# Turning w_out in 32 by 32 blocks on VectorE instead of 128 by 128 on TensorE

## The chip, the cores and the metric

The kernel runs on one core of one Trainium2 chip. The metric is the device time in microseconds (us) of one execution, lower is better. A core has five engines that run their own instruction streams in order and wait for each other by semaphores: TensorE (PE in the profile, with its weight loads shown apart as PEld), VectorE (DVE), ScalarE (ACT), GpSimd (POOL) and SyncE (SP). Here SP does nothing but issue transfers to 16 DMA engines; an "SPq" row is such an issue.

## The reference

```python
# 1. attention with mixing over heads, before and after the softmax: q, k, v are [4, 12, 448, 64]
scores = einsum(scale * q @ k.T, w_pre); attn = softmax(scores); attn = einsum(attn, w_post)
x = (attn @ v) as [1792, 768]
# 2. a wide layer: w_in [768, 2048], w_out [2048, 768]
h = x @ w_in
g = h * cos(h)
x = g @ w_out
# 3. soft mixture: phi [768, 32], 8 experts of 4 slots, w1 [8, 768, 1024], w2 [8, 1024, 768]
logits = x @ phi
d = softmax(logits, over the tokens);  slot_in = d.T @ x
slot_out = per expert: relu(slot_in @ w1) @ w2
out = softmax(logits, over the slots) @ slot_out          # [1792, 768] float32
```

The kernel never forms g @ w_out for all tokens. Logits are g @ (w_out @ phi), so it needs the small product W = w_out @ phi ([2048, 32]), and for that product w_out with its 768 columns on the partitions, that is, turned. The rest of w_out is used only after the sum over the tokens.

## The kernel before

**Phase A** (`phase_a`) is the attention. A planner (`Plan`) with costs and due times sets its order. It also narrows w_in and w_out from their stored form to float32 copies in DRAM. Phase A is untouched by the change.

**Phase B** (`phase_b`) is the wide layer, the logits and the sum over tokens. It takes 1792 tokens in four blocks of 512, 512, 512 and 256, and in each block 16 slices of 128 of the 2048 hidden columns: `body(v)` for v = 0 to 63, written out in a fixed order. "Slice v" below means one `body(v)`. In a slice, `l1(v)` (lines 700 to 710) makes h with 18 matmuls on PE: w_in and x are each split in a high and a low part. The split of the weights for slice v + 2 (`split_w`, lines 650 and 651) is one pass on ACT and one on DVE. `act` and `act2` (lines 717 to 729) make g = h cos(h): ACT line 720, DVE lines 721 and 723, ACT line 728, DVE line 729. `consume` (line 750) turns g of slice v - 2 in 32 by 32 blocks on DVE. After each fourth slice `logits` (line 757) multiplies four g tiles by four tiles of W on PE; that of slices 4i to 4i + 3 stands in slice 4i + 5.

W is made during block 0, in four pieces `fb` of 512 rows of w_out each. The table `more` (line 866) says in which slice which step stands:

- `load_wo(fb)` loads 512 rows of w_out, rows on the partitions.
- `turn_wo(fb, half)` (line 665) turns 384 columns: 12 transposes of 128 by 128 on PE into PSUM (line 672), and three copies of 128 by 512 out of it, on DVE (line 675) or ACT (line 677). There are eight such calls, in slices 1 to 8.
- `mul_phi(fb)` (line 681) multiplies by phi into `pw` on PE; ACT copies it to `ws` (line 690).
- `turn_w(fb)` (line 692) turns the product on PE into a PSUM tile, also called `wtr`, and DVE copies it to `W` (line 697, `wphi` in the profile).

In the table the four `turn_w` stand in slices 4, 6, 8 and 10, and the `logits` that use them in 5, 9, 13 and 17. Steps of `more` come after `split_w` and before `consume`, `logits` and `act2` of the same slice. Block 0 ends with slice 15; the last `logits` of the block is in slice 17.

**Phase C** (`phase_c`) is the experts and the output. It streams w1 and w2 through a ring of buffers; 18 of its 64 units are loaded from slice 16 on, 12 of them into `early`, the same memory that `phase_b` calls `room`.

Of the kernel before, what the change touches and what calls it, by code (L numbers as in the profile page):

```python
# [9 lines left out]
F32 = mybir.dt.float32  # L10
# [9 lines left out]
EARLY, RING, NWF, NWH, LAG = 12, 3, 4, 2, 2  # L20
# [580 lines left out]
def phase_b(tc, st, consts, ident, xT_d, w_in, w_out, phi, sums, room, x0, ahead):  # L601
# [6 lines left out]
    nc = tc.nc  # L608
    SIZES = [512, 512, 512, 256]
    NB = len(SIZES)  # L610
    with ExitStack() as ctx:
# [39 lines left out]
            nc.vector.tensor_tensor(out=wf_t[v], in0=wf_t[v].bitcast(F32), in1=wh.bitcast(F32), op=ALU.subtract)  # L651
            wh_t[v] = wh

        wo_t, wt_t = {}, {}
        ws, ph = room[7][:, :512], room[7][:, 512:704].rearrange("p (c s) -> p c s", c=6)

        def load_wo(fb):
            wo_t[fb] = []
            for i in range(2):
                t = room[2 * (fb % 2) + i].rearrange("p (t d) -> p t d", t=2)  # L660
                r0 = 512 * fb + 256 * i
                nc.sync.dma_start(out=t, in_=w_out[r0:r0 + 256].rearrange("(t p) d -> p t d", p=128))
                wo_t[fb].append(t)

        def turn_wo(fb, half):

            wt = wt_t[fb, half] = room[4 + (2 * fb + half) % 3].rearrange("p (c f) -> p c f", c=3)
            for c in range(3):
                pt = p1.tile([128, 512], F32, tag="tr", bufs=4, name=f"wtr{fb}_{half}_{c}")
                cols = slice(384 * half + 128 * c, 384 * half + 128 * c + 128)  # L670
                for t in range(4):
                    nc.tensor.transpose(pt[:, t * 128:(t + 1) * 128],  # L672
                                        wo_t[fb][t // 2][:, t % 2, cols], ident)
                if c % 2 != half:
                    nc.vector.tensor_copy(out=wt[:, c], in_=pt)
                else:
                    nc.scalar.copy(out=wt[:, c], in_=pt)
            if half and fb + 2 < 4:
                load_wo(fb + 2)

        def mul_phi(fb):
            pw = p1.tile([128, 512], F32, tag="tr", bufs=4, name=f"pw{fb}")
            wt = [wt_t[fb, c // 3][:, c % 3] for c in range(6)]
            for c in range(4):
                nc.tensor.matmul(pw[32 * c:32 * c + 32], ph[:, c, :], wt[c], start=True, stop=False)
            for r in range(4):
                c, cols = 4 + r // 2, slice(256 * (r % 2), 256 * (r % 2) + 256)
                nc.tensor.matmul(pw[32 * r:32 * r + 32, cols], ph[:, c, :], wt[c][:, cols],
                                 start=False, stop=True)
            nc.scalar.copy(out=ws, in_=pw)  # L690

        def turn_w(fb):
# [34 lines left out]
        def act2(h, r):  # L727
            nc.scalar.activation(out=r, in_=r, func=AF.Sin, scale=-2.0 * math.pi, bias=hpi)
            nc.vector.tensor_tensor(out=r, in0=h, in1=r, op=ALU.mult)
# [119 lines left out]
        for part in range(3):  # L849
# [4 lines left out]
        cT, g_acc, z_acc, gn_all, x1, cg = sums  # L854
# [3 lines left out]
        W = sp.tile([128, 16, 32], F32, name="wphi")  # L858
        m_acc = sp.tile([128, 1], F32, name="m_acc")
        magic, hpi = consts[:, 0:1], consts[:, 1:2]  # L860
        nc.sync.dma_start(out=ph, in_=phi.rearrange("(c p) s -> p c s", p=128))
        load_wo(1)

        g_t = {}

        more = {1: [(turn_wo, 0, 0)], 2: [(turn_wo, 0, 1)], 3: [(mul_phi, 0), (turn_wo, 1, 0)],
                4: [(turn_w, 0), (turn_wo, 1, 1)], 5: [(mul_phi, 1), (turn_wo, 2, 0)],
                6: [(turn_w, 1), (turn_wo, 2, 1)], 7: [(mul_phi, 2), (turn_wo, 3, 0)],
                8: [(turn_w, 2), (turn_wo, 3, 1)], 9: [(mul_phi, 3)], 10: [(turn_w, 3)]}


        def body(v):

            b, f = divmod(v, 16)
            last = v - LAG if v - LAG < V - 4 else -1
            pt = l1(v)
            for _ in range(AHEAD_AT.count(v)):
                ahead.pop(0)()
            if v + NWF < V:
                load_w(v + NWF)  # L880
            g_t[v] = act(v, pt)
            if v + 2 < V:
                split_w(v + 2)
            for f_, *x in more.get(v, ()):
                f_(*x)
            if last >= 0:
                after(last)
            act2(*g_t[v])
            if last >= 0:
                soft(last)  # L890
            if f == 0 and b + 1 < NB:
                load_x(b + 1)
            if f in (7, 9, 11) and b + 1 < NB:
                split_x(b + 1, (f - 7) // 2)
# [20 lines left out]
        for v in range(V):  # L915
            body(v)
# [253 lines left out]
@with_exitstack  # L1170
def tile_kernel(ctx: ExitStack, tc: tile.TileContext, q, k, v, w_pre, w_post, w_in, w_out, phi, w1, w2, out):
    nc = tc.nc
    B, H, S, D = q.shape
    const = ctx.enter_context(tc.tile_pool(name="const", bufs=1))
    dram = ctx.enter_context(tc.tile_pool(name="dram", bufs=1, space=DRAM))
    with tc.manual_schedule():
        ident = const.tile([128, 128], F32, name="ident")
        make_identity(nc, ident)
        xT_d = dram.tile([H * D, B * S], F32, name="xT_d")
        wide, narrow = [], []  # L1180
        for i, w in enumerate((w_in, w_out)):
            r = w.shape[0] // 128
            d = dram.tile(list(w.shape), F32, name=f"w32_{i}")
            wide.append((w.rearrange("(p r) f -> p (r f)", p=128),
                         d.rearrange("(p r) f -> p (r f)", p=128)))
            narrow.append(d)
        keep, nexts, sums, loads, rest, wo, gu, x0s = [], [], [], [], [], [], [], []
        xp = ctx.enter_context(ExitStack())

        def start_b():  # L1190
            pool = ctx.enter_context(tc.tile_pool(name="keep", bufs=1, reuse_waits="tile"))

            consts = pool.tile([128, 2], F32, name="consts")
            nc.vector.memset(consts[:, 0:1], MAGIC)
            nc.vector.memset(consts[:, 1:2], math.pi / 2)
            st4 = pool.tile([128, 32], F32, name="st4")
            st = pool.tile([128, 128], F32, name="st")

            early = [pool.tile([128, 1536], F32, name=f"early{i}") for i in range(EARLY)]
            x0 = xp.enter_context(tc.tile_pool(name="x0", bufs=1, reuse_waits="tile")).tile(  # L1200
                [128, 2, 3072], F32R, name="x0")
            nc.vector.tensor_reduce(out=st4, in_=ident.rearrange("p (a s) -> p s a", a=4), axis=AX.X, op=ALU.add)
            nc.vector.tensor_copy(out=st.rearrange("p (a s) -> p a s", a=4),
                                  in_=st4.unsqueeze(1).to_broadcast([128, 4, 32]))
            keep.extend([st, wo, early, gu, rest, xp.close])
            x0s.append(x0)
            nexts.append(phase_b(tc, st, consts, ident, xT_d, narrow[0], narrow[1], phi, sums, early, x0,
                                 loads))
            next(nexts[0])

        phase_a(tc, ident, q, k, v, w_pre, w_post, xT_d, wide, start_b)
        pool = ctx.enter_context(tc.tile_pool(name="sums", bufs=1, side="right", reuse_waits="tile"))

        cg = pool.tile([128, 3072], F32, name="cg")
        sums.append(pool.tile([128, B * S // 128, 32], F32, name="cT"))
        sums.append(pool.tile([128, w_in.shape[1] // 4], F32, name="g_acc"))
        sums.append(pool.tile([128, 1], F32, name="z_acc"))
        gn_all = pool.tile([128, 12288], F32, name="gn")
        x1 = pool.tile([128, 2, 3072], F32R, name="x1")
        sums.extend([gn_all, x1, cg])  # L1220

        early, x0 = keep[2], x0s[0]
        gu.append(cg[:, 1536:3072])
        gu.extend(gn_all[:, c:c + 1536] for c in range(0, 7680, 1536))
        x1s = [x1[:, i, c:c + 768].bitcast(F32) for c in (1536, 2304, 0, 768) for i in range(2)]
        wo.extend(x1s[:4])
        wo.extend(x0[:, i // 4, 768 * (i % 4):768 * (i % 4) + 768].bitcast(F32) for i in range(8))
        wo.extend(x1s[4:])
        first = [(lambda i=i, t=t: load_unit(nc, t, unit_source(w1, w2, i))) for i, t in enumerate(early + gu)]
        rows = [(lambda i=i, t=t: nc.sync.dma_start(out=t, in_=narrow[1][128 * i:128 * i + 128]))  # L1230
                for i, t in enumerate(wo)]
        loads.extend(first[:EARLY] + rows[:12] + first[EARLY:])
        rest.extend(rows[12:])
        for _ in nexts[0]:
            pass
        phase_c(tc, ident, *sums, w1, w2, *keep, out)
# [31 lines left out]
```

## Time and profile before

| | us |
|---|---|
| median of 3 runs | 917.29 |
| lowest and highest run | 914.87 and 920.3 |
| profiled execution, its own time | 911.71 |
| its span, first to last instruction | 909.9 |
| slices 0 to 17, from the first matmul of slice 0 to the first of slice 18 | 498.00 to 596.86 |

The profile is of one execution; all times inside it are from the start of its span. In that execution PE was busy 95% of the span, DVE 68%, ACT 57%. A row of a timeline gives the start, the length, the engine, the line, the operation, and what it writes and reads; a bracket at its end is the idle time of the engine before it and what ended that. Consecutive instructions overlap a little in such rows, so what an instruction costs its engine is read from start to start.

### The profile page before, as it was taken

What the parts mean: (1) busy time and instruction counts of PE and PEld (TensorE: products, weight loads), DVE (VectorE), ACT (ScalarE), POOL (GpSimd) and SP (SyncE); (2) the same over time, 40 slices, a digit from 0 to 9 for tenths busy, and PEclk for the clock granted to TensorE, in tenths of its full rate; (3) what the DMA queues carried; (4) which work ended last, traced back from release to release, by engine and by line L of the source; (5) the groups of instructions that cost most, each with busy time, mean ns of one, the idle gap of its engine ahead of it and who ended that gap; (6) DMA issues with size and microseconds to landing.
All of it is one profiled execution on the core that took longest, in us unless ns stands there. A gap on an engine that the chain in (4) does not pass through costs nothing.

```text
span 909.9 us, 17966 instructions
## 1 busy us (share of the span) xinstructions
PE 866.6 (95%) x6732; PEld 612.4 (67%) x6732; DVE 620.6 (68%) x1282; ACT 519.4 (57%) x1146; POOL 178.8 (20%) x272
## 2 busy tenths in 40 slices
PE   7899999999999999999999999999999999989665
PEld 5567777776777777677778877776777777833112
DVE  4568878688879788778744657777877788833003
ACT  5667767677767678657655545455546457512003
POOL 2233344343434334334310000000000000010000
PEclk9999999999999999999999999999999999999867
DMA  7999896999878997979419732363563358979998
GB/s 167 194 208 246 209 244 203 218 218 276 213 205 224 253 214 177 248 205 250 117 47 289 229 122 70 110 237 129 164 221 132 121 175 276 307 307 414 416 375 314
DMA packets 175474, 198.93 MB, mean 219 GB/s; under 512 B 73424, under 2 KB 147090, under 8 KB 175388
## 3 DMA queue, kind: packets, MB, share of 16 engines
q1 hardware_dynamic: 158504, 159.18, 58.5%
q0 software_dynamic: 14272, 37.96, 18.3%
q8 instruction: 53, 0.87, 0.4%
q10 hardware_dynamic: 2612, 0.65, 0.3%
q14 instruction: 33, 0.27, 0.1%
HBM read 135.40 MB, written 23.59 MB: 175 GB/s over the span
## 4 chain that ended last, share of the span: by engine, by line
PE 81%; DMA 11%; DVE 2%; SPq 1%; issue 1%; ACT 1%; POOL 0%; ACTq 0%; DVEq 0%; POOLq 0%
PE po L444 16%; PE pre L406 15%; PE h L706 9%; PE av L468 8%; PE h L707 8%; PE h L709 8%; PE s L359 8%; DMA early<-in_moe_w_dram 4%; DMA s<-ss 4%; PE p L818 2%; DMA cg<-in_moe_w_dram 2%; DMA ring<-in_moe_w_dram 2%; PE lg L757 1%; PE kt L293 1%; PE wtr L672 1%
## 5 line engine op out<-in xcount | busy, mean ns | idle before, releaser
L444 PEld LDWEIGHTS po<-wc,e 120*112 120x112 f32 x1440 | 170.5, 177 | 56.3 <-issue 41.5
L444 PE MATMUL po<-wc,e 120*112 120x120 f32 x1440 | 182.8, 269 | 0.5 <-ACT am L229 0.5
L406 PE MATMUL pre<-s,kron_pre 120*120 120x448 f32 x360 | 166.5, 552 | 4.6 <-issue 2.7
L409 DVE TENSOR_REDUCE mz<-pre 120x1 f32<-120x448 f32 x180 | 111.1, 620 | 45.6 <-PE pre L406 44.6
L379 POOL DMA_DIRECT2D s<-ss x180 | 107.0, 597 | 174.5 <-ACT ss L229 120.1
L706 PE MATMUL h<-x,wh 128*128 128x512 f32 (+1 forms) x384 | 139.1, 372 | 0.1
L707 PE MATMUL h<-x,wh 128*128 128x512 f32 (+1 forms) x384 | 135.7, 363 | 0.0
L413 ACT ACTIVATE e<-pre,mz 120x448 f32<-120x448 f32 x180 | 114.6, 637 | 29.2 <-DVE mz L409 26.4
L229 ACT COPY am<-po 112x360 f32<-112x360 f32 x190 | 87.4, 461 | 65.3 <-PE po L444 63.3
L706 PEld LDWEIGHTS h<-x,wh 128*128 128x128 f32 x384 | 72.2, 188 | 26.4 <-ACT cg L720 10.0
L709 PE MATMUL h<-x,wf 128*128 128x512 f32 (+1 forms) x384 | 87.3, 363 | 0.0
L720 ACT ACTIVATE cg<-h 128x512 int32<-128x512 f32 (+1 forms) x64 | 34.6, 541 | 90.7 <-PE h L709 89.5
L543 POOL TENSOR_TENSOR nar<-nar,cvt 128x384 uint32<-128x384 uint32 x64 | 64.1, 1001 | 98.1 <-DVE cvt L534 42.0
L468 PE MATMUL av<-am,v 112*64 112x120 f32 (+1 forms) x1536 | 83.0, 262 | 0.0
L468 PEld LDWEIGHTS av<-am,v 112*64 112x64 f32 x1536 | 74.0, 137 | 10.4 <-issue 4.9
L707 PEld LDWEIGHTS h<-x,wh 128*128 128x128 f32 x384 | 72.2, 188 | 11.2
L721 DVE SCALAR_TENSOR_TENSOR cg<-h,cg 128x512 f32<-128x512 f32 (+1 forms) x64 | 39.8, 621 | 57.2 <-ACT cg L720 55.2
L709 PEld LDWEIGHTS h<-x,wf 128*128 128x128 f32 x384 | 66.3, 188 | 11.8
L1037 POOL MEMSET own<- 128x192 f32 x2 | 0.4, 252 | 347.6 <-PE si L1023 347.6
L229 ACT COPY ss<-s 120x448 f32<-120x448 f32 (+1 forms) x104 | 54.1, 532 | 25.0 <-PE s L359 15.5
L406 PEld LDWEIGHTS pre<-s,kron_pre 120*120 120x120 f32 x360 | 53.2, 184 | 21.9 <-issue 16.1
L651 DVE TENSOR_TENSOR wf<-wf,wh 128x768 fp32r<-128x768 f32 x64 | 60.9, 951 | 8.7 <-ACT wh L650 8.7
(174 smaller groups left out, 1223.3 us busy)
## 6 DMA issues: line engine op xcount, KB each, us to landing
s<-ss POOLq DMA_DIRECT2D x144, 210.0 KB, 7.5
early<-in_moe_w_dram SPq DMA_DIRECT2D x36, 768.0 KB
wf<-w SPq DMA_DIRECT2D x64, 384.0 KB
raw<-in_moe_w_in_dram SPq DMA_DIRECT2D x32, 384.0 KB
w<-nar SPq DMA_DIRECT2D x64, 192.0 KB
raw<-in_moe_w_out_dram SPq DMA_DIRECT2D x32, 384.0 KB
gn<-in_moe_w_dram SPq DMA_DIRECT2D x16, 768.0 KB
early<-w SPq DMA_DIRECT2D x8, 768.0 KB
```

The lines of the kernel that those rows point to most:

```text
L229: nc.scalar.copy(out=out, in_=in_)
L359: nc.tensor.matmul(pts[o][:n, :S], x[r, p, :n], y[r, p, :], start=(i == 0), stop=(i == 2))
L379: QUEUE[e].dma_start(out=s2t[ti][h::12, :n // 10], in_=x[o][:n])
L406: nc.tensor.matmul(prt[gi, c][:, :S], kpre, s2t[ti][:, 3 * g + c, :], start=True, stop=True)
L409: nc.vector.tensor_reduce(out=mz[gi][:, 0, c:c + 1], in_=prt[gi, c][:, :S], axis=AX.X, op=ALU.max, negate=True)
L413: nc.scalar.activation(out=et[gi][:, c, :], in_=prt.pop((gi, c))[:, :S], func=AF.Exp, bias=mz[gi][:, 0, c:c + 1], accum_out=mz[gi][:, 1, c ...
L444: nc.tensor.matmul(pt[:, :360].rearrange("p (g i) -> p g i", i=30)[:, :, 10 * c:10 * c + 10], et[gi][:, c, jt * CJ:(jt + 1) * CJ], wct[gi] ...
L468: nc.tensor.matmul(pt[64 * o:64 * o + 64, x * 120:x * 120 + n], vt[:, g, jt, :], am[ti % 2][:, g, jt, :n], start=(jt == 0), stop=(jt == NJ ...
L543: nc.gpsimd.tensor_tensor(out=f, in0=f, in1=x["t"], op=ALU.add)
L706: nc.tensor.matmul(pt, wh[:, c], xh[:, c, :], start=(c == 0), stop=False)
L707: nc.tensor.matmul(pt, wh[:, c], xl[:, c, :], start=False, stop=False)
L709: nc.tensor.matmul(pt, wl[:, c], xh[:, c, :], start=False, stop=(c == 5))
```

## The change

w_out is now turned by DVE in blocks of 32 by 32 and no longer by PE. For such a turn to give w_out with columns on partitions, the load puts column quarter a (192 columns) on partitions 32a to 32a + 31: four transfers for each piece, each to 32 partitions, in runs of 192 elements (768 bytes), where there were two transfers of whole rows (3072 bytes) to all 128 partitions. `turn_wo(fb, x)` is one DVE instruction on 128 by 768; it stands in slice 4 fb + x, after `act2`, so there is one in each of slices 0 to 15. phi is loaded in the matching order, in four transfers. `mul_phi` reads the turned tile with a stride. `mul_phi(fb)` now stands in slice 4 fb + 4 and `turn_w(fb)` in slice 4 fb + 5. The `early` tiles become one tile `room`, with w_out in columns of its own for each piece, and `ws` and `ph` move into a part of `gn_all` that block 0 does not use.

```diff
-        def turn_wo(fb, half):
-            wt = wt_t[fb, half] = room[4 + (2 * fb + half) % 3].rearrange("p (c f) -> p c f", c=3)
-            for c in range(3):
...
-                    nc.tensor.transpose(pt[:, t * 128:(t + 1) * 128],
-                                        wo_t[fb][t // 2][:, t % 2, cols], ident)
-                if c % 2 != half:
-                    nc.vector.tensor_copy(out=wt[:, c], in_=pt)
-                else:
-                    nc.scalar.copy(out=wt[:, c], in_=pt)
-            if half and fb + 2 < 4:
-                load_wo(fb + 2)
+        def load_wo(fb):
+            src = w_out[512 * fb:512 * fb + 512].rearrange("(r i) (a d) -> a i r d", i=32, a=4)
+            for a in range(4):
+                nc.sync.dma_start(out=wo_src(fb)[32 * a:32 * a + 32], in_=src[a])
+        def turn_wo(fb, x):
+            if x == 0:
+                c = 1536 * (8 + 2 * (fb % 2))
+                wt_t[fb] = room[:, c:c + 3072]
+            cols = slice(768 * x, 768 * x + 768)
+            nc.vector.transpose(out=wt_t[fb][:, cols], in_=room[:, 3072 * fb:3072 * fb + 3072][:, cols])
...
+            wt = wt_t[fb].rearrange("p (r c i) -> p c r i", c=6, i=32)
...
-        nc.sync.dma_start(out=ph, in_=phi.rearrange("(c p) s -> p c s", p=128))
-        load_wo(1)
+        ws, ph = gn_all[:, 7168:7680], gn_all[:, 7680:7872].rearrange("p (c s) -> p c s", s=32)
+        for a in range(4):
+            nc.sync.dma_start(out=ph[32 * a:32 * a + 32],
+                              in_=phi[192 * a:192 * a + 192].rearrange("(c j) s -> j c s", j=32))
...
-        more = {1: [(turn_wo, 0, 0)], 2: [(turn_wo, 0, 1)], 3: [(mul_phi, 0), (turn_wo, 1, 0)],
...
+        more = {}
+        for fb in range(4):
+            more[4 * fb + 4] = [(mul_phi, fb)]
+            more[4 * fb + 5] = [(turn_w, fb)]
+        for fb in range(1, 4):
+            more[2 * fb - 1] = more.get(2 * fb - 1, []) + [(load_wo, fb)]
...
             act2(*g_t[v])
+            if v < 16:
+                turn_wo(v // 4, v % 4)
```

On PE before, `turn_w(0)` follows slice 4 and the `logits` that use it follow slice 5 (`h4`, `h5`: the matmuls of these slices; `wtr0_6189`: the PSUM tile of `turn_w`; the other `wtr` tiles: transposes of w_out; `lg0`: the logits).

```order
L709 MATMUL h4_6164<-x0_5873,wf0_5879 128x512 x6
L695 MATMUL wtr0_6189<-st_5857,early7_5865 128x32 x4
L672 MATMUL wtr1_1_0_6195<-ident_62,early2_5860 128x128 x2
...
L709 MATMUL h5_6218<-x0_5873,wf1_5880 128x512 x6
L685 MATMUL pw1_6243<-early6_5864,early7_5865 32x512 x3
...
L672 MATMUL wtr2_0_0_6253<-ident_62,early0_5858 128x128 x2
...
L757 MATMUL lg0_6272<-cg_5967,wphi_5982 32x512 x4
```

On PE of the changed kernel, whose lines from 655 on have smaller numbers (709 is 701, 695 is 687, 757 is 749, 685 is 677), the same stretch holds:

```order
L701 MATMUL h4_6102<-x0_5862,wf0_5868 128x512 x6
L677 MATMUL pw0_6127<-early_5858,gn_5962 32x512 x4
L680 MATMUL pw0_6127<-early_5858,gn_5962 32x256 x4
...
L701 MATMUL h5_6141<-x0_5862,wf1_5869 128x512 x6
L687 MATMUL wtr0_6166<-st_5857,gn_5962 128x32 x4
L749 MATMUL lg0_6177<-cg_5958,wphi_5973 32x512 x4
L698 MATMUL h6_6185<-x0_5862,wh0_5871 128x512
```

The transposes of w_out are gone, `mul_phi` has moved one slice down, and `turn_w` stands directly ahead of the `logits` that read its result.

On DVE before, the copy to W of `turn_w(0)` is in slice 4 (from the reading of `h4` on):

```order
L721 SCALAR_TENSOR_TENSOR cg_5967<-h4_6164,cg_5967 128x512
L723 TENSOR_SCALAR cg_5967<-cg_5967 128x512
L651 TENSOR_TENSOR wf2_5881<-wf2_5881,wh0_5882 128x768
L697 COPY wphi_5982<-wtr0_6189 128x128
L675 COPY early4_5862<-wtr1_1_0_6195 128x512
L675 COPY early4_5862<-wtr1_1_2_6207 128x512
L750 STREAM_TRANSPOSE gn_5971<-cg_5967 128x512
L729 TENSOR_TENSOR cg_5967<-h4_6164,cg_5967 128x512
```

In the changed kernel DVE's slices 3 (its end), 4 (its start) and 5 read as follows; lines 713, 715, 742, 721 and 689 are 721, 723, 750, 729 and 697 of before, and 671 is the new turn.

```order
L742 STREAM_TRANSPOSE gn_5962<-cg_5958 128x512
L721 TENSOR_TENSOR cg_5958<-h3_6069,cg_5958 128x512
L671 STREAM_TRANSPOSE early_5858<-early_5858 128x768
L713 SCALAR_TENSOR_TENSOR cg_5958<-h4_6102,cg_5958 128x512
...
L713 SCALAR_TENSOR_TENSOR cg_5958<-h5_6141,cg_5958 128x512
L715 TENSOR_SCALAR cg_5958<-cg_5958 128x512
L651 TENSOR_TENSOR wf3_5872<-wf3_5872,wh1_5873 128x768
L689 COPY wphi_5973<-wtr0_6166 128x128
L742 STREAM_TRANSPOSE gn_5962<-cg_5958 128x512
L721 TENSOR_TENSOR cg_5958<-h5_6141,cg_5958 128x512
L671 STREAM_TRANSPOSE early_5858<-early_5858 128x768
```

The fourth turn of a piece is DVE's last instruction of a slice, and `mul_phi` on PE needs it one slice later. The copy to W is DVE's fourth instruction of slice 5, behind three that need `h5`.

## Rows read from the trace of the kernel before

**Rows 1.** Slices 0 to 17: length, busy PE, PEld, DVE, ACT, POOL, clock, DMA, GB/s.

```profile
498.00:596.86 98.86, 98.86 (x550) 76.42 (x548) 68.03 (x107) 49.23 (x77) 0.00 (x0) 1.00 0.47 147
```

**Rows 2.** Timeline of PE: start us, us, engine, line, operation.

```profile
498.00 0.50 PE L706 MATMUL h<-x,wh 128*128 128x512 f32 x1
...
524.23 0.97 PE L695 MATMUL wtr<-st,early 128*128 128x32 f32 x8
525.03 1.51 PE L672 MATMUL wtr<-ident,early 128*128 128x128 f32 x12
526.30 0.48 PE L706 MATMUL h<-x,wh 128*128 128x512 f32 x1
...
530.57 1.06 PE L685 MATMUL pw<-early,early 128*32 128x512 f32 x8
...
532.00 1.53 PE L672 MATMUL wtr<-ident,early 128*128 128x128 f32 x12
533.46 1.07 PE L757 MATMUL lg<-cg,wphi 128*32 128x512 f32 x8
534.45 0.50 PE L706 MATMUL h<-x,wh 128*128 128x512 f32 x1
...
538.67 0.97 PE L695 MATMUL wtr<-st,early 128*128 128x32 f32 x8
...
569.83 0.39 PE L706 MATMUL h<-x,wh 128*128 128x512 f32 x1
...
573.91 0.39 PE L706 MATMUL h<-x,wh 128*128 128x512 f32 x1
...
596.86 0.51 PE L706 MATMUL h<-x,wh 128*128 128x512 f32 x1
```

**Rows 3.** Timeline of DVE in slice 4.

```profile
525.05 0.69 DVE L721 SCALAR_TENSOR_TENSOR cg<-h,cg 128x512 f32<-128x512 f32 x1 [2.83 <-ACT cg L720]
...
526.99 0.28 DVE L697 COPY wphi<-wtr 128x128 f32<-128x128 f32 x1
527.19 1.28 DVE L675 COPY early<-wtr 128x512 f32<-128x512 f32 x2
528.39 0.70 DVE L750 STREAM_TRANSPOSE gn<-cg 128x512 f32<-128x512 f32 x1
```

**Rows 4.** Timeline of DVE in slice 15, which has no extra work.

```profile
592.40 0.69 DVE L721 SCALAR_TENSOR_TENSOR cg<-h,cg 128x512 f32<-128x512 f32 x1 [0.98 <-ACT cg L720]
...
594.97 0.65 DVE L729 TENSOR_TENSOR cg<-h,cg 128x512 f32<-128x512 f32 x1
596.60 0.69 DVE L721 SCALAR_TENSOR_TENSOR cg<-h,cg 128x512 f32<-128x512 f32 x1 [0.99 <-ACT cg L720]
```

**Rows 5.** Groups by line, shapes apart: DVE's 32 by 32 turns of g (busy, mean ns).

```profile
L750 DVE STREAM_TRANSPOSE gn<-cg 128x512 f32<-128x512 f32 x48 | 33.8, 703 | 0.0
L750 DVE STREAM_TRANSPOSE gn<-cg 128x256 f32<-128x256 f32 x16 | 6.9, 434 | 0.0
```

**Rows 6.** Timelines of DVE and PEld at a wait of PE for DVE.

```profile
516.35 0.65 DVE L729 TENSOR_TENSOR cg<-h,cg 128x512 f32<-128x512 f32 x1
...
517.30 0.16 PEld L685 LDWEIGHTS pw<-early,early 128*32 128x32 f32 x8 [0.35 <-DVE cg L729]
```

**Rows 7.** Groups by line: matmuls of 512 columns, read with a stride (818) and without (834).

```profile
L818 PE MATMUL p<-gn 32*32 32x512 f32 x384 | 13.4, 597 | 0.0
L834 PE MATMUL ps<-gn,st 128*32 128x512 f32 x30 | 4.7, 604 | 0.1
```

**Rows 8.** Issue of w_out's first piece, DMA totals of 486 to 500 us, end of slice 0 on DVE.

```profile
486.36 0.87 SPq L662 DMA_DIRECT2D early<-w  x2
487.27 1.39 SPq L644 DMA_DIRECT2D wf<-w  x2
...
DMA packets 3565, 4.09 MB, mean 292 GB/s; under 512 B 1014, under 2 KB 2550, under 8 KB 3563
...
508.21 0.69 DVE L729 TENSOR_TENSOR cg<-h,cg 128x512 f32<-128x512 f32 x1 [0.68 <-ACT cg L728]
```

More of the change, by code (lines that the diff above doesn't have):

```diff
@@ L652, in split_w, with wo_src @@
             wh_t[v] = wh
-        wo_t, wt_t = {}, {}
-        ws, ph = room[7][:, :512], room[7][:, 512:704].rearrange("p (c s) -> p c s", c=6)
+        wt_t = {}
+        def wo_src(fb):
+            return room[:, 3072 * fb:3072 * fb + 3072].rearrange("p (r d) -> p r d", r=16)
         def load_wo(fb):
[L658 to L663, printed above, removed]
@@ L665, in turn_wo @@
-        def turn_wo(fb, half):
-            wt = wt_t[fb, half] = room[4 + (2 * fb + half) % 3].rearrange("p (c f) -> p c f", c=3)
-            for c in range(3):
-                pt = p1.tile([128, 512], F32, tag="tr", bufs=4, name=f"wtr{fb}_{half}_{c}")
-                cols = slice(384 * half + 128 * c, 384 * half + 128 * c + 128)
-                for t in range(4):
-                    nc.tensor.transpose(pt[:, t * 128:(t + 1) * 128],
-                                        wo_t[fb][t // 2][:, t % 2, cols], ident)
-                if c % 2 != half:
-                    nc.vector.tensor_copy(out=wt[:, c], in_=pt)
-                else:
-                    nc.scalar.copy(out=wt[:, c], in_=pt)
-            if half and fb + 2 < 4:
-                load_wo(fb + 2)
+            src = w_out[512 * fb:512 * fb + 512].rearrange("(r i) (a d) -> a i r d", i=32, a=4)
@@ L681, in mul_phi @@
+            for a in range(4):
[6 more added lines that the diff above has]
+            nc.vector.transpose(out=wt_t[fb][:, cols], in_=room[:, 3072 * fb:3072 * fb + 3072][:, cols])
         def mul_phi(fb):
             pw = p1.tile([128, 512], F32, tag="tr", bufs=4, name=f"pw{fb}")
-            wt = [wt_t[fb, c // 3][:, c % 3] for c in range(6)]
+            wt = wt_t[fb].rearrange("p (r c i) -> p c r i", c=6, i=32)
@@ L684, in mul_phi @@
             for c in range(4):
-                nc.tensor.matmul(pw[32 * c:32 * c + 32], ph[:, c, :], wt[c], start=True, stop=False)
+                nc.tensor.matmul(pw[32 * c:32 * c + 32], ph[:, c, :], wt[:, c], start=True, stop=False)
             for r in range(4):
-                c, cols = 4 + r // 2, slice(256 * (r % 2), 256 * (r % 2) + 256)
-                nc.tensor.matmul(pw[32 * r:32 * r + 32, cols], ph[:, c, :], wt[c][:, cols],
-                                 start=False, stop=True)
+                c, half = 4 + r // 2, r % 2
@@ L690, in mul_phi @@
+                nc.tensor.matmul(pw[32 * r:32 * r + 32, 256 * half:256 * half + 256], ph[:, c, :],
+                                 wt[:, c, 8 * half:8 * half + 8], start=False, stop=True)
             nc.scalar.copy(out=ws, in_=pw)
@@ L860, in phase_b @@
         magic, hpi = consts[:, 0:1], consts[:, 1:2]
-        nc.sync.dma_start(out=ph, in_=phi.rearrange("(c p) s -> p c s", p=128))
-        load_wo(1)
+        ws, ph = gn_all[:, 7168:7680], gn_all[:, 7680:7872].rearrange("p (c s) -> p c s", s=32)
+        for a in range(4):
+            nc.sync.dma_start(out=ph[32 * a:32 * a + 32],
+                              in_=phi[192 * a:192 * a + 192].rearrange("(c j) s -> j c s", j=32))
         g_t = {}
-        more = {1: [(turn_wo, 0, 0)], 2: [(turn_wo, 0, 1)], 3: [(mul_phi, 0), (turn_wo, 1, 0)],
-                4: [(turn_w, 0), (turn_wo, 1, 1)], 5: [(mul_phi, 1), (turn_wo, 2, 0)],
-                6: [(turn_w, 1), (turn_wo, 2, 1)], 7: [(mul_phi, 2), (turn_wo, 3, 0)],
-                8: [(turn_w, 2), (turn_wo, 3, 1)], 9: [(mul_phi, 3)], 10: [(turn_w, 3)]}
+        more = {}
[4 more added lines that the diff above has]
+            more[2 * fb - 1] = more.get(2 * fb - 1, []) + [(load_wo, fb)]
         def body(v):
@@ L1197, in start_b @@
             st = pool.tile([128, 128], F32, name="st")
-            early = [pool.tile([128, 1536], F32, name=f"early{i}") for i in range(EARLY)]
+            room = pool.tile([128, EARLY * 1536], F32, name="early")
+            early = [room[:, 1536 * i:1536 * i + 1536] for i in range(EARLY)]
             x0 = xp.enter_context(tc.tile_pool(name="x0", bufs=1, reuse_waits="tile")).tile(
@@ L1206, in start_b @@
             x0s.append(x0)
-            nexts.append(phase_b(tc, st, consts, ident, xT_d, narrow[0], narrow[1], phi, sums, early, x0,
+            nexts.append(phase_b(tc, st, consts, ident, xT_d, narrow[0], narrow[1], phi, sums, room, x0,
                                  loads))
```

## The prediction

> **What bounds the kernel now.** I read the summary of the page first (PE busy 95% of the span), then the chain of work that ended last, which through phase B is a string of PE's own matmuls, and then the stretch that the change touches: slices 0 to 17, from the first matmul of slice 0 to the first of slice 18. The busy times by stretch [rows 1] show PE busy in all 98.86 us of it, at the full granted clock of 1.00, with DVE at 68 us, ACT at 49 us and the DMA engines at 0.47. So what PE is rid of there is worth its whole length, unless PE begins to wait. From slice 18 on the order of all engines is the same in both kernels, and the loads for phase C hang on slice numbers; a shift at slice 18 arrives at the end as it is. I forecast that shift.
>
> **What PE is rid of, and what is left.** The reader is to see four lengths on PE's timeline [rows 2]. A slice that follows a slice takes 573.91 - 569.83 = 4.08 us. One that follows other work takes longer: 538.67 - 534.45 = 4.22, so 0.14 more (the one from 526.30 to 530.57 takes 4.27, part of it a short wait). `turn_w` takes 525.03 - 524.23 = 0.80, `mul_phi` 532.00 - 530.57 = 1.43, `logits` 534.45 - 533.46 = 0.99. The twelve transposes of one `turn_wo` take 526.30 - 525.03 = 1.27; there are eight calls, about 10.2 us. With the transposes gone the stretch holds 18 slices at 4.08 = 73.4, eight entries after other work or after the start at 0.14 = 1.1, and four times 1.43 + 0.80 + 0.99 = 12.9: together 87.4 us. If PE never waited, the change would be worth 98.9 - 87.4 = 11.4 us (the transposes, and fewer entries and short waits around them).
>
> **What DVE gets.** Eight calls of `turn_wo` gave DVE twelve copies of about 0.60 each, from start to start (the two in [rows 3] take 528.39 - 527.19 = 1.20). They go: 7.2 us. Sixteen turns of 128 by 768 come. The trace has turns of 512 and 256 columns at 0.703 and 0.434 us [rows 5]; another 256 columns cost 0.269, so 768 cost 0.97, and 0.89 from start to start, as rows overlap by some 0.08. Bounds: not under 0.70, the price of 512 columns, and not over 1.41, two turns of 512. Sixteen are 14.2 us. In a plain slice DVE's own work takes from 592.40 to 594.97 + 0.65, 3.22 us, and it idles 0.98 in a period of 4.20 [rows 4]. The turn fits that hole almost exactly: DVE needs 4.1 us a slice against PE's 4.08. It becomes as full as PE in plain slices, but not more; the time that PE spends on `mul_phi`, `turn_w` and `logits` lets it catch up. ACT loses twelve copies, which is worth nothing, since it idles anyway.
>
> **The two new waits on PE.** The order on PE and DVE shows them, the trace prices them. Let T be the moment when PE has finished a slice's matmuls and goes on.
>
> The second wait is the large one. In slice 4 fb + 5 PE does `turn_w`, and directly behind it `logits`, which read the W that DVE must first copy out. DVE cannot be early with that copy: it stands behind line 721 (713 now), which reads this same slice's h. In slice 4 of before, T is 524.23, line 721 starts at 525.05 (0.82 after T, since ACT's line 720 comes between), and the copy to W runs from 526.99 to 527.27, 3.04 after T [rows 2, 3]. DVE idled before it, so this is the shortest it can be. From DVE's end to PE's start I add 0.2: the trace has one such wait, 0.30 from 517.00 to 517.30 [rows 6], which is the upper bound; the lower is 0. PE's own `turn_w` covers 0.80 of it. PE stands idle 3.04 + 0.20 - 0.80 = 2.44 us, four times. Before, the copy had a slice or more between it and its reader. Queued behind the waiting `logits` are all of PE's later slices.
>
> The first wait: `mul_phi(fb)` follows the matmuls of slice 4 fb + 4 and needs the fourth turn of its piece, DVE's last instruction of slice 4 fb + 3. With T of that slice, DVE starts at T + 0.82, works 3.22 less an overlap of 0.07, and turns for 0.97: done at T + 4.94, seen at T + 5.14. PE is there at T + 4.08. It waits 1.06, if DVE has no lag. Lag comes from the splits of x on DVE (slices 7, 9 and 11, after the turn) and from the start of the phase; the idle 2.44 us of PE let DVE recover before each next group, so I take none.
>
> Together 3.50 a group, 14.0 for four (12.4 with no hop, 14.8 with 0.30). The stretch becomes 87.4 + 14.0 = 101.4, against 98.9: **2.5 us slower**. Of the forecast's own uncertainty, the turn's price moves the first wait one for one (0.27 less at 0.70, 0.44 more at 1.41, and in that last case a lag as well), and a lag of 2 us from slice 0 would lengthen the first of the four.
>
> **Edits at no cost.** The strided reading in `mul_phi`: 597 ns for strided and 604 for plain matmuls of 512 columns [rows 7]; at most 0.1 us either way. The load of phi now waits for the last use of phase A's memory and holds SP's queue up to about 498; the load behind it is that of slice 4's weights, which needs slice 0 finished at about 502 anyway, and if that cover were gone there are still two slices until it is needed. Issues: SP has eight more for w_out (16 against 8) and three more for phi, at 0.87 for two [rows 8], 4.8 us spread over six slices, in which SP mostly waits for PE to free a weight buffer; without that cover each would delay the weights of a slice by 0.44, which are loaded four slices ahead. The second piece of w_out is no longer loaded ahead of phase A's last stores, which can let slice 0's ACT work start earlier; PE does not wait for that, so zero.
>
> **Time.** The profiled execution took 911.71 us (span 909.9); with 2.5 more, 914.2. The median of the runs, 917.29, is 5.6 above it, so the runs should give 917.29 + 2.5 = 919.8. About 0.5% (4.6 us) is what a measurement of this kernel can tell from no change.
>
> **Rivals.** (a) *PE does not wait.* Then all 11.4 us are gained: 905.9. For it: PE bounds the stretch without a gap [rows 1], and DVE has 30 us idle. Against it: W is read directly behind its making, and the copy cannot precede line 721 of the same slice. If only the wait before `logits` were much shorter than read, say 1 us, the gain is 3 us, still within the 0.5%. I give it 0.08. The Trainium skill, "VectorE: DVE Perf Modes", section "Rules for kernel authors", says that for a 32 by 32 turn DVE's transpose is the fastest path; taken as the whole story it argues for (a). The trace agrees on the instruction (0.97 us of DVE by my working for what takes PE half of 1.27 us and 1.5 copies), but the rule prices the engines' work and not the waits.
>
> (b) *The quarter loads come late.* The first piece, 1.57 MB, is issued from 486.36 on, in a stretch that moves 292 GB/s [rows 8]: 5.4 us, landed at about 493. The first turn would stand at the end of slice 0 on DVE, behind line 729 of 508.21 [rows 8], or some 2 us earlier if ACT starts earlier. At half the rate it lands at about 498, at a quarter at about 508: the rival decides from there. Beyond that DVE stalls at its first turn with everything of slices 1 and on behind it, the weights of slices 2 and 3, issued behind w_out, come late too, and PE, which can run about two slices ahead, stops. At a sixth of the rate (32 us, 519) DVE is 10 us late and PE some 6, and the later pieces cost as much again: 919.8 + 8 = 928. Against it: the rate would have to fall far. Chance 0.12. The Trainium skill, "SBUF — State Buffer", section "Door 1: The DMA port swizzle (why `[64,N]` ≈ `[32,N]`)", says that a transfer to 32 partitions reaches only 8 of the 16 ports, and that two transfers to different partitions do not add up. By that rule the piece would take about twice as long, 11 us as an estimate, and land at about 498; no row before shows a load to 32 partitions.
>
> (c) *The turn is dearer than its columns*, near 1.3 us. DVE then needs 4.4 us in a slice, falls 0.3 behind in each, and the first wait of each group grows by about 0.35 + 1.0: four times that is 5 us more, 924.9. Nothing in the rows speaks for it but that 768 columns do not occur. Chance 0.10.
>
> **Chances.** Forecast 0.70, (a) 0.08, (b) 0.12, (c) 0.10. The forecast's 2.5 us lies under the 4.6 of the bound; with its spread and that of the runs (914.87 to 920.3) I split its 0.70 into 0.02 faster, 0.56 same and 0.12 slower. With (a) faster, (b) slower and (c) 0.04 same and 0.06 slower: faster 0.10, same 0.60, slower 0.30. The forecast alone spans 916 to 924; with part of (b) and (c) the range is 912 to 926.
>
> **What would show it.** In the profile after: no PE transposes of w_out; sixteen turns of 128 by 768 on DVE near 0.97; PEld idle before the `logits` of slices 5, 9, 13 and 17, released by DVE's copy to W, about 2.4 each; PE idle before `mul_phi`, released by the turn, about 1.1 each; slice 18 some 101.4 us after slice 0. It is wrong if PE has no gap there, if the turn misses 0.97 by over 0.2, if DVE waits for a DMA at a turn, or if phase C differs by more than the shift.

## The result, and the profile after

The changed kernel took 929.71 us (median of 4 runs, 928.5 to 930.41) against 918.79 for the kernel before (4 runs, 914.87 to 922.0): ratio 1.0122, 95% interval 1.0084 to 1.0159. It is 1.2% slower, about 11 us; forecast were 2.5 us, and the time lies above the stated range.

The profiled execution starts slice 0 at 504.70, not at 498.00. Phase A is the same program in both, and over the twelve kernels told of here that start lies between 498.0 and 506.2 without regard to the change. So all comparisons below are made from the first matmul of slice 0 to the first of slice 18, the stretch of [rows 1]. From slice 18 to the end before takes 313.0 us and after 314.6; the other kernels here, with the same order in that part, take 313.0 to 317.5.

Busy time by stretch of the changed kernel (columns as in [rows 1]): the whole stretch, and two pieces behind its first `logits`, in slices 6 and 7.

```profile
504.70:613.65 108.95, 95.37 (x455) 69.97 (x453) 76.85 (x115) 44.29 (x66) 0.00 (x0) 0.94 0.67 158
539.06:543.96 4.90, 4.90 (x16) 3.89 (x13) 0.15 (x1) 0.00 (x0) 0.00 (x0) 0.55 1.18 223
544.00:548.00 4.00, 4.00 (x19) 3.34 (x18) 1.81 (x3) 1.98 (x3) 0.00 (x0) 1.00 1.13 192
```

The stretch is 10.1 us longer than in [rows 1]. PE is idle for 108.95 - 95.37 = 13.6 us of it, where it was never idle before, and the mean granted clock is 0.94, where it was 1.00. Behind the first `logits` the clock is 0.55 for 4.9 us and then 1.00 again. What PE waited for in the stretch (total us, times, longest):

```profile
PE lg L749 <- DVE wphi L689: 10.0, 4, 3.6
PE pw L677 <- DVE early L671: 3.5, 4, 1.2
```

These are the two waits of the forecast and no other. PE's timeline (columns as in [rows 2]) from the `mul_phi` of slice 4 into slice 6, and then the later `logits` with the first matmul behind each:

```profile
526.60 1.07 PE L677 MATMUL pw<-early,gn 128*32 128x512 f32 x8 [1.19 <-DVE early L671]
...
528.03 0.50 PE L698 MATMUL h<-x,wh 128*128 128x512 f32 x1
...
530.89 1.52 PE L701 MATMUL h<-x,wf 128*128 128x512 f32 x6
532.50 1.08 PE L687 MATMUL wtr<-st,gn 128*128 128x32 f32 x8
537.20 1.94 PE L749 MATMUL lg<-cg,wphi 128*32 128x512 f32 x8 [3.62 <-DVE wphi L689]
539.06 0.80 PE L698 MATMUL h<-x,wh 128*128 128x512 f32 x1
539.65 0.63 PE L699 MATMUL h<-x,wh 128*128 128x512 f32 x1
540.08 0.63 PE L698 MATMUL h<-x,wh 128*128 128x512 f32 x1
...
543.49 0.40 PE L698 MATMUL h<-x,wh 128*128 128x512 f32 x1
543.73 0.40 PE L699 MATMUL h<-x,wh 128*128 128x512 f32 x1
543.96 1.52 PE L701 MATMUL h<-x,wf 128*128 128x512 f32 x6
...
560.04 0.97 PE L687 MATMUL wtr<-st,gn 128*128 128x32 f32 x8
563.15 1.19 PE L749 MATMUL lg<-cg,wphi 128*32 128x512 f32 x8 [2.13 <-DVE wphi L689]
564.26 0.80 PE L698 MATMUL h<-x,wh 128*128 128x512 f32 x1
...
568.56 1.54 PE L701 MATMUL h<-x,wf 128*128 128x512 f32 x6
...
587.85 1.93 PE L749 MATMUL lg<-cg,wphi 128*32 128x512 f32 x8 [2.13 <-DVE wphi L689]
589.71 0.80 PE L698 MATMUL h<-x,wh 128*128 128x512 f32 x1
...
593.30 1.53 PE L701 MATMUL h<-x,wf 128*128 128x512 f32 x6
...
612.65 1.07 PE L749 MATMUL lg<-cg,wphi 128*32 128x512 f32 x8 [2.13 <-DVE wphi L689]
613.65 0.50 PE L698 MATMUL h<-x,wh 128*128 128x512 f32 x1
```

Read the starts. Behind the first wait the `logits` take 539.06 - 537.20 = 1.86 us, where [rows 2] have 0.99, and a matmul of 512 columns starts every 0.43 (539.65 to 540.08); from 543.49 on it is 0.24. Nothing about these instructions has changed but the clock: 1.2 GHz instead of 2.4. It happens behind three of the four waits; behind the fourth the `logits` take 1.00.

DVE ahead of that first `logits`, from the turn to the copy to W, and then two of its rows ahead of the second:

```profile
534.07 0.96 DVE L671 STREAM_TRANSPOSE early<-early 128x768 f32<-128x768 f32 x1
534.96 0.65 DVE L713 SCALAR_TENSOR_TENSOR cg<-h,cg 128x512 f32<-128x512 f32 x1
535.64 0.43 DVE L715 TENSOR_SCALAR cg<-cg 128x512 uint32<-128x512 uint32 x1
535.99 0.95 DVE L651 TENSOR_TENSOR wf<-wf,wh 128x768 fp32r<-128x768 f32 x1
536.86 0.28 DVE L689 COPY wphi<-wtr 128x128 f32<-128x128 f32 x1
...
560.87 0.69 DVE L713 SCALAR_TENSOR_TENSOR cg<-h,cg 128x512 f32<-128x512 f32 x1 [1.42 <-ACT cg L712]
...
562.81 0.28 DVE L689 COPY wphi<-wtr 128x128 f32<-128x128 f32 x1
```

In the first group DVE is late and has no gap; the copy stands fourth in its slice, as read from the order. PE, with its product ready at about 533.6, waits for the copy at 536.86. In the second group DVE had been idle 1.42 us, so it is not late; the copy ends at 563.09 and `logits` start at 563.15. Of the three instructions ahead of the copy only two need the h of this slice: line 651 splits the weights of a later one and stands there by order alone. No run here puts the copy ahead of it.

### The profile page after: what moved, and what is told of

It reads as the page before. It is cut to its first block, busy times and chain, and to the rows that moved or that the text cites. A ratio compares the mean times of both kernels' runs of the same rounds, so it can differ in the third digit from the quotient of the medians.

```text
span 928.2 us, 17766 instructions
## 1 busy us (share of the span) xinstructions
PE 867.9 (94%) x6636; PEld 609.2 (66%) x6636; DVE 626.9 (68%) x1286; ACT 513.5 (55%) x1134; POOL 179.1 (19%) x272
## 4 chain that ended last, share of the span: by engine, by line
PE 76%; DMA 11%; DVE 6%; SPq 3%; ACT 2%; issue 1%; DVEq 0%; ACTq 0%
PE po L444 15%; PE pre L406 14%; PE av L468 8%; PE h L698 7%; PE h L699 7%; PE s L359 7%; PE h L701 6%; DMA knat<-in_k_dram 4%; DMA early<-in_moe_w_dram 3%; PE eh L1060 2%; DMA wf<-w 2%; PE p L810 2%; DMA ring<-in_moe_w_dram 2%; PE lg L749 2%; DVE wf L651 2%
## 5 line engine op out<-in xcount | busy, mean ns | idle before, releaser
L698 PE MATMUL h<-x,wh 128*128 128x512 f32 (+1 forms) x384 | 142.6, 381 | 0.0
L699 PE MATMUL h<-x,wh 128*128 128x512 f32 (+1 forms) x384 | 138.8, 371 | 0.0
L698 PEld LDWEIGHTS h<-x,wh 128*128 128x128 f32 x384 | 74.6, 194 | 30.2 <-issue 8.0
L699 PEld LDWEIGHTS h<-x,wh 128*128 128x128 f32 x384 | 74.6, 194 | 11.7
```

The costliest lines, as they stand in the source:

```text
L698: nc.tensor.matmul(pt, wh[:, c], xh[:, c, :], start=(c == 0), stop=False)
L699: nc.tensor.matmul(pt, wh[:, c], xl[:, c, :], start=False, stop=False)
```

## The experiments

The theory after the result: the waits are as forecast, and the half clock that follows them is the rest of the loss. Two rivals: the rest comes from the late quarter loads, or from DVE, which is full of turns. All medians stand beside runs of the kernel before on the same chip (917.52, 917.08 and 917.29 in the three groups).

**The wait kept, PE kept busy in it.** Behind `turn_w` PE turns the identity 18 times into an unused PSUM tile.

```diff
-            more[4 * fb + 5] = [(turn_w, fb)]
+            more[4 * fb + 5] = [(turn_w, fb), (fill, 18)]
```

> The changed kernel, with 18 transposes of the identity into a spare PSUM tile put on TensorE between turn_w and the logits that wait for W (slices 5, 9, 13 and 17; about 2 us of work in a wait of 2.1 to 3.6). Theory (clock): the wait itself costs some 13.5 us in all, and the rest of the loss is TensorE at half clock after three of these waits (6.8 + 3.4 + 3.4 us at a granted clock of 0.5, half of which is lost). With TensorE busy in the wait the clock stays at 1.0, the time falls by about 7 us, from 930 to 923, and no slice of slices 5 to 18 has matmuls of 0.43 us. Rival (loads): the rest of the loss comes from weights that arrive late behind the quarter loads of w_out; then filling the wait changes nothing, 929 to 931.

921.11 us, ratio 1.0037 (0.9993 to 1.0080). The stretch:

```profile
498.62:600.35 101.73, 97.07 (x526) 74.23 (x525) 76.99 (x115) 44.51 (x66) 0.00 (x0) 1.00 0.70 170
```

PE's timeline in slice 5 of this kernel:

```profile
525.74 0.97 PE L687 MATMUL wtr<-st,gn 128*128 128x32 f32 x8
526.55 2.16 PE L864 MATMUL fill<-ident 128*128 128x128 f32 x18
530.04 1.06 PE L749 MATMUL lg<-cg,wphi 128*32 128x512 f32 x8 [1.33 <-DVE wphi L689]
531.04 0.50 PE L698 MATMUL h<-x,wh 128*128 128x512 f32 x1
```

The `logits` still cannot start before the copy to W (4.30 us from `turn_w`, 4.70 in the changed kernel), but the clock stays at 1.00, and the stretch is 7.2 us shorter. It is 101.73, where the forecast's sum at full clock was 101.4. Loads and turns of this kernel are those of the changed one, so neither rival can account for the 7.2, but for some 0.9 by which waits are shorter: 0.40 here, and 0.5 before the four `mul_phi` (2.9 in all, 3.5 in the changed kernel). The other 6.3 us are the clock.

**The new places with the old turns.** The kernel before, its steps put where the change puts them.

```diff
...
+        for fb in range(4):
+            more[4 * fb + 2] = [(turn_wo, fb, 0)]
+            more[4 * fb + 3] = [(turn_wo, fb, 1)]
+            more[4 * fb + 4] = [(mul_phi, fb)]
+            more[4 * fb + 5] = [(turn_w, fb)]
```

> The kernel before with w_out turned on TensorE as before, but with the steps where the change puts them: turns in slices 4fb+2 and 4fb+3, mul_phi in 4fb+4, turn_w in 4fb+5, directly ahead of the logits that read its result. Theory (placement and clock): four waits of 2.3 us before the logits, 9 us, and about 7 us of half clock after them, although nothing is turned on VectorE and nothing is loaded by quarters: 919 + 16 = 935, slower than the changed kernel. Rival (loads): only the 9 us of waits, 928, and the clock stays at 1.0. Rival (VectorE's turns or the quarter loads make the whole loss): 919.

932.24 us, ratio 1.0169 (1.0115 to 1.0223), stretch 112.63, clock 0.95. PE's waits in it, and two of its `logits`:

```profile
PE lg L757 <- DVE wphi L697: 8.5, 4, 2.1
```

```profile
537.74 1.94 PE L757 MATMUL lg<-cg,wphi 128*32 128x512 f32 x8 [2.13 <-DVE wphi L697]
...
565.57 1.06 PE L757 MATMUL lg<-cg,wphi 128*32 128x512 f32 x8 [2.13 <-DVE wphi L697]
```

Whole rows in two loads a piece, no turn of w_out on DVE, and still the wait of 2.13 and the half clock: the placement alone does it. The stretch is 3.7 us longer than in the changed kernel: PE still makes the transposes, while `mul_phi` does not wait and a spell at half clock is missing. The wait is the same 2.13 before both rows, and only the first is followed by half clock. What decides between them is open.

**One slice earlier.** The changed kernel, with `mul_phi` and `turn_w` one slice up and the turns moved up to suit (two in slice 1), so that the copy to W has a slice before its reader.

```diff
-            more[4 * fb + 4] = [(mul_phi, fb)]
-            more[4 * fb + 5] = [(turn_w, fb)]
+            more[4 * fb + 3] = [(mul_phi, fb)]
+            more[4 * fb + 4] = [(turn_w, fb)]
...
-            if v < 16:
-                turn_wo(v // 4, v % 4)
+            for i in [0] if v == 0 else [1, 2] if v == 1 else [v + 1] if v < 15 else []:
+                turn_wo(i // 4, i % 4)
```

> The changed kernel with all its steps one slice earlier: turn 0 in slice 0, turns 1 and 2 in slice 1, turn i in slice i - 1 from then on, mul_phi in 4fb+3, turn_w in 4fb+4, so that the copy to W has a slice before the logits. Theory (placement and clock): the four waits before the logits (10.0 us) and the half clock after them (6.8 us) go, the wait before mul_phi (3.5 us) stays: 930 - 17 = 913, faster than before. Rival (loads): the waits go, but weights still come late and the first turn of the next piece now meets its load, so 919 to 922, with VectorE waiting for DMAs. If the order had nothing to do with it: 930.

915.82 us, ratio 0.9974 (0.9938 to 1.0010); stretch 95.82. The wait of `logits` is gone. 915.82 cannot be told from the kernel before. Left is the wait of `mul_phi`, and behind its longest, 2.44, PE is at half clock again (clock 0.98):

```profile
PE pw L677 <- DVE early L671: 5.2, 4, 2.4
```

**The load in another cut.** Sixteen transfers of 32 rows to all 128 partitions, in place of four to 32 partitions.

```diff
-            for a in range(4):
-                nc.sync.dma_start(out=wo_src(fb)[32 * a:32 * a + 32], in_=src[a])
+            for r in range(16):
+                r0 = 512 * fb + 32 * r
+                nc.sync.dma_start(out=wo_src(fb)[:, r], in_=w_out[r0:r0 + 32].rearrange("i (a d) -> a i d", a=4))
```

> The changed kernel with each piece of w_out loaded in 16 transfers of 32 rows to all 128 partitions instead of four transfers of 512 rows to 32 partitions each; the runs of 768 bytes and the place of everything stay. Theory (placement and clock): the loads cost only the late weights of slice 6 (first wait before logits 3.6 instead of 2.1 us), so about 1.5 us less, 928, and that only if transfers to 128 partitions are faster; the waits and the half clock stay. Rival (loads to 32 partitions run at half rate and this makes the rest of the loss): DMA engines move w_out at 300 GB/s and more instead of about 200, and the time falls by 7 us, to 922. If the rate hangs on the 768-byte runs, it stays at 200 GB/s and 930.

965.77 us, ratio 1.0530 (1.0468 to 1.0592); stretch 146.61. It failed as a cure, against the 922 to 930 expected, and shows what a really late load costs: PE waits 12.4 us for weights and 20.1 for ACT's copy of `pw`, ahead of which ACT stands for weights too. The DMA engines at 492 to 506 us (totals, then the sync engine's queue: packets, MB, share of 16 engines):

```profile
DMA packets 1572, 1.21 MB, mean 87 GB/s; under 512 B 65, under 2 KB 1568, under 8 KB 1568
...
q1 hardware_dynamic: 1549, 1.15, 27.3%
```

A good quarter of the engines' time (27.3%) is used, and the rate is 87 GB/s. The Trainium skill, "DMA: Bandwidth & Descriptors", section "Why a DMA increments its semaphore by 16 and not by 1", says that a transfer uses the largest number of engines up to 16 that divides the slowest dimension of both of its sides; the source here begins with 4. The trace agrees.

**Turns ahead of the slice's other steps.** As one slice earlier, but the turn stands right behind `split_w`, ahead of `more`.

```diff
+            for i in [0] if v == 0 else [1, 2] if v == 1 else [v + 1] if v < 15 else []:
+                turn_wo(i // 4, i % 4)
             for f_, *x in more.get(v, ()):
...
-            if v < 16:
-                turn_wo(v // 4, v % 4)
```

> The changed kernel with its steps one slice earlier (as in the run before) and, on VectorE, each turn put right behind the split of the weights, ahead of the turn of g and the last product of the slice. Theory (placement and clock): the last turn of a piece now ends some 0.3 us before TensorE asks for it, so the waits before mul_phi (5.2 us in the run with the steps one slice earlier, 1.7 us of half clock behind the longest) shrink to what the load of the second piece causes: 916 - 5 = 911, faster than the kernel before by 0.5 to 1%. Rival (VectorE is now the bound): the products that release TensorE's PSUM come 0.9 us later in each slice, TensorE waits for them, no gain: 916 or more.

914.44 us where 911 was expected, ratio 0.9960 (0.9934 to 0.9986); stretch 94.19. The wait of `mul_phi` falls to one of 1.4; now one `logits` waits 2.2, behind a turn for which DVE waited 5.0 for its load, and half clock follows it.

**The loads further apart.** The same, with the loads of pieces 1 to 3 in slices 0, 3 and 7, where they stood in 1, 3 and 5.

```diff
-            more[2 * fb - 1] = more.get(2 * fb - 1, []) + [(load_wo, fb)]
+            at = {1: 0, 2: 3, 3: 7}[fb]
+            more[at] = more.get(at, []) + [(load_wo, fb)]
```

> As the run with early turns, with the loads of pieces 1, 2 and 3 in slices 0, 3 and 7 instead of 1, 3 and 5. Theory (placement, clock, and loads only as a small term): no wait of VectorE for a load and no wait of TensorE in slices 0 to 17 is left, the stretch takes 87.5 to 88.5 us against 98.9 before, granted clock 1.00 in it, and the time is 918 - 11 = 907. Rival (the loads keep all DMA engines busy from slice 0 to 8 at half rate and weights come late wherever they stand): the stretch keeps waits for weights, 911 or more.

916.26 us where 907 was expected, ratio 0.9968 (0.9937 to 0.9999); stretch 93.78. No gain over the last: one wait of 2.9 is left, of `turn_w` for ACT, and ACT itself stood 6.7 for a slice's weights, queued behind other loads. Half clock follows here too, but only about 2 us after PE has resumed:

```profile
525.28 1.08 PE L687 MATMUL wtr<-st,gn 128*128 128x32 f32 x8 [2.95 <-ACT gn L682]
...
527.82 0.63 PE L698 MATMUL h<-x,wh 128*128 128x512 f32 x1
```

**Partition groups alone.** The kernel before, each load of w_out cut in four by partitions, rows still whole.

```diff
-                nc.sync.dma_start(out=t, in_=w_out[r0:r0 + 256].rearrange("(t p) d -> p t d", p=128))
+                src = w_out[r0:r0 + 256].rearrange("(t p) d -> p t d", p=128)
+                for a in range(4):
+                    nc.sync.dma_start(out=t[32 * a:32 * a + 32], in_=src[32 * a:32 * a + 32])
```

> The kernel before, its loads of w_out (whole rows, runs of 3072 bytes) cut in four transfers, each to a group of 32 partitions. It tells what halves the rate of the loads in the changed kernel. If the 32 partitions do: while w_out's first piece moves, all DMA engines are busy at about 190 GB/s. If the 768-byte runs do: 300 to 400 GB/s, as before. Time: as before, 916 to 921, by either, since TensorE has the piece only to use from slice 1 on; 925 if late weights cost much.

Its result stands beside that of the next run.

**Short runs alone.** The kernel before, each load cut in four by columns, 768-byte runs to all 128 partitions.

```diff
+                    nc.sync.dma_start(out=t[:, :, 192 * a:192 * a + 192], in_=src[:, :, 192 * a:192 * a + 192])
```

> The kernel before, its loads of w_out cut in four transfers by column quarters: runs of 768 bytes, each transfer to all 128 partitions. If the 768-byte runs halve the rate: about 190 GB/s while the first piece moves; if the 32 partitions do: 300 GB/s or more. Time: as before, 916 to 921.

918.12 us, ratio 1.0006 (0.9977 to 1.0035), and 918.13, ratio 1.0006 (0.9981 to 1.0031); stretches 98.87 and 99.89 (in the second PE waits once, 0.8 us, for weights). No cost in time that could be measured, but the rates differ. DMA totals while w_out moves, in the kernel before (489 to 492) and with partition groups (497 to 500):

```profile
DMA packets 432, 1.20 MB, mean 399 GB/s; under 512 B 23, under 2 KB 46, under 8 KB 432
```

```profile
DMA packets 273, 0.68 MB, mean 228 GB/s; under 512 B 55, under 2 KB 55, under 8 KB 272
```

Groups of 32 partitions, with the same long runs, bring 399 GB/s down to 228; short runs alone to 274 (489 to 493); the changed kernel, with both, moves 203 (495 to 503). The forecast's rule of the Trainium skill ("SBUF — State Buffer", "Door 1: The DMA port swizzle (why `[64,N]` ≈ `[32,N]`)") agrees with the first.

**Earlier, and the loads out of each other's way.** As with the loads further apart, but in slices 0, 4 and 8, and the load of x for block 1 in slice 3 and not 0.

```diff
-            at = {1: 0, 2: 3, 3: 7}[fb]
+            at = {1: 0, 2: 4, 3: 8}[fb]
...
-            if f == 0 and b + 1 < NB:
+            if f == (0 if b else 3) and b + 1 < NB:
```

> As the run with spread loads (steps one slice earlier, turn behind the split), with the load of x for block 1 moved from slice 0 to slice 3 and w_out's pieces 1, 2, 3 loaded in slices 0, 4 and 8. In the run with spread loads ScalarE waited 6.7 us for the weights of slice 6, which stood in the DMA queues behind x and a quarter-loaded piece; TensorE then waited 3 us for ScalarE's copy of pw and ran at half clock for 3.4 us: 93.8 us for slices 0 to 17. Theory: these are the only losses left, so the stretch takes 88 to 89 us at a granted clock of 1.00, 10 less than before, and the time is 907 to 909 (ratio 0.989 to 0.992). Rival (half-rate loads make weights late wherever they stand): some wait for weights stays in the stretch, 92 us or more, ratio 0.996 as in the last two.

910.18 us, ratio 0.9922 (0.9893 to 0.9952): faster than both kernels, by a little less than expected. The stretch, and PE around slice 5:

```profile
502.45:591.91 89.46, 88.94 (x454) 66.06 (x452) 72.69 (x110) 42.14 (x63) 0.00 (x0) 1.00 0.74 175
```

```profile
524.68 0.97 PE L687 MATMUL wtr<-st,gn 128*128 128x32 f32 x8
525.49 0.48 PE L698 MATMUL h<-x,wh 128*128 128x512 f32 x1
...
529.75 1.06 PE L749 MATMUL lg<-cg,wphi 128*32 128x512 f32 x8
```

A slice now lies between `turn_w` and `logits`, and one wait of 0.5 is left in the whole stretch. 89.46 is 2.1 us above the forecast's 87.4 for a PE that never waits; 0.5 of that is the wait.

**The spread loads alone.** The changed kernel with that load of x, and pieces 1 to 3 in slices 0, 5 and 9.

```diff
-            more[2 * fb - 1] = more.get(2 * fb - 1, []) + [(load_wo, fb)]
+            at = {1: 0, 2: 5, 3: 9}[fb]
+            more[at] = more.get(at, []) + [(load_wo, fb)]
...
```

> The changed kernel with every step where the change has it, only its loads are spread: x for block 1 in slice 3, w_out's pieces 1, 2, 3 in slices 0, 5 and 9. It sizes the late weights by themselves. Theory (placement and clock): the first wait before the logits is 2.1 us as the other three, instead of 3.6; the other waits and the half clock after some of them stay; the stretch takes 107 us and the time is 928. Rival (loads): the stretch comes near 101, the sum without clock and late loads, 922.

930.61 us, ratio 1.0122 (1.0085 to 1.0160), stretch 108.05, clock 0.95: the time of the changed kernel. PE's waits:

```profile
PE lg L749 <- DVE wphi L689: 8.5, 4, 2.1
PE pw L677 <- DVE early L671: 6.2, 4, 3.9
```

ACT ahead of that 3.9:

```profile
519.49 0.83 ACT L650 CAST wh<-wf 128x768 fp32r<-128x768 f32 x1 [3.39 <-DMA wf<-w]
```

All four waits of `logits` are now 2.13, so the 3.62 of the changed kernel's first was the loads (ACT stood 5.1 us there for a slice's weights). But weights are late here too, one slice earlier: ACT stands 3.39, DVE's turn behind it is late, and one wait of `mul_phi` is 3.90 instead. So this run moves the long wait and does not remove it. What the changed kernel would take with no late weights at all, no run here shows.

## Why the forecast was wrong

*What PE is rid of: right.* No transpose of w_out is left on PE. Without waits and at full clock the stretch takes 89.46, one wait of 0.5 in it; forecast 87.4.

*The turn: right.* In the groups by line of the changed kernel, beside [rows 5]:

```profile
L671 DVE STREAM_TRANSPOSE early<-early 128x768 f32<-128x768 f32 x16 | 15.3, 959 | 0.0
```

0.96 us where 0.97 was worked out, so rival (c) is out.

*The two waits: right in cause and place, near in size.* The profile has 3.62 once and 2.13 three times before `logits`, and 0.71 to 1.19 before `mul_phi`: 13.5 us of idle time. The forecast's 14.0 is counted from start to start, and in that measure the ends of PE's rows come on top, 1.4 us (worked out below): 14.9. Without lag, `logits` start 563.15 - 560.04 - 0.80 = 2.31 after the end of `turn_w`, where 2.44 was forecast: the copy ends 3.05 after T, as forecast (3.04), but the hop to PE is 0.06 and not 0.20. The excess is the lag in the first wait, 1.5 us, a term that the forecast put at nothing. Rival (a) is out by the same rows.

*The step that failed: the sum, "87.4 + 14.0 = 101.4".* It took every matmul at the length it has in [rows 2], that is, at the full clock of a PE that is never idle, and then put idle time between them. In the rows above, three spells at half clock cost: `logits` 0.87, 0.12 and 0.87 over 0.99; the slice behind them up to line 701 takes 4.90, 4.30 and 3.59, where one at full clock takes 2.86 (528.03 to 530.89), so 2.04, 1.44 and 0.73. That is 6.1 us. With it the sum is 87.4 + 13.5 + 6.1 = 107.0 of 108.95. Of the last 1.9, some 1.4 are the ends of PE's rows, which the next matmul covers only where there is no wait (`turn_w` takes 0.97 ahead of a wait and 0.80 without, 0.17 in each of eight); 0.5 stays unexplained. Keeping PE busy in the wait gives 101.73, so the step is shown by a run and not only argued. None of the three rivals held this case: all priced a wait at its own length.

*Rival (b): right in the rate, wrong in its weight.* The loads run at about half rate. What that does to the queue is in SP's issues and one split on ACT, in the changed kernel:

```profile
513.61 6.22 SPq L663 DMA_DIRECT2D early<-w  x4
519.94 4.73 SPq L644 DMA_DIRECT2D wf<-w  x2
```

```profile
531.13 0.83 ACT L650 CAST wh<-wf 128x768 fp32r<-128x768 f32 x1 [5.08 <-DMA wf<-w]
```

The four issues of a piece, costed at 1.7 us (twice the 0.87 of [rows 8]), take 6.2 here, the weights of a slice are issued behind them, and ACT waits 5.1 for weights: the source of the 1.5 us of lag above. Spreading the loads in the changed kernel moved that lag and left the stretch at 108.05. With the steps one slice earlier, spreading them brought it from 93.78 to 89.46.

*Edits at no cost: right but for one.* Groups and short runs in the kernel before cost nothing that could be measured there, and the strided matmuls of `mul_phi` take 1.07 for eight where [rows 2] have 1.06. Only the eight more issues on SP had a price, the one just told.

## What to carry to other kernels

Where TensorE is the bound and has been busy throughout, price a new wait on it at its length plus what may follow at half clock; here 13.5 us of waits took about 6 us more with them. Work taken off the bounding engine pays only if what it feeds is made early: the change with W read directly behind its making was 1.2% slower. A slice between the two made up for the loss (ratio 0.9974, not to be told from the kernel before); 0.8% faster came only with the turn earlier in its slice and the loads moved apart as well. If a step cannot be moved, matmuls whose result nobody reads can keep the clock up in the wait; here they did.

## What the hardware showed that was not expected

- In slices 0 to 17 half clock came behind waits of 2.1 us and more (up to 3.9, but for the run with sixteen transfers, which has longer ones), and behind none of 1.4 or less. It did not come behind each of 2.1: behind three of four in the changed kernel, and behind one wait of 2.13 and not another in the same run.
- With w_out in four groups of 32 partitions the DMA engines read as busy nearly throughout (all nines at 495 to 503 in the changed kernel) at 203 GB/s, as they do with whole rows at 399; a full DMA row does not tell the rate.
- A source pattern that begins with a dimension of 4 used a good quarter of the DMA engines' time, 87 GB/s.
